# The first loads of an attention kernel issued from two queues, with new issue costs in its planner

## The chip, the cores and the metric

The kernel runs on one core of a Trainium2 chip. The metric is the device time of one execution in microseconds (us). Three runs of the kernel before took 1328.55, 1330.45 and 1333.21 us, so the median is 1330.45 us. All times of single operations below come from one profiled execution, which took 1330.71 us, of which its trace spans 1329.0 us.

The engines are called as the profile calls them: PE is the matrix engine (PEld its weight loads), DVE the vector engine, ACT the scalar engine, POOL the general one, and SP the engine that here does nothing but issue DMAs. A DMA is issued by an engine's instruction stream, in order, and then moves its bytes on the core's 16 DMA engines while the issuing engine goes on.

## The reference

Attention whose heads are mixed before and after the softmax ("talking heads"), then two layers of dense work. The sizes are 4 batches, 12 heads, 448 positions, 64 features a head.

```python
scores = scale * np.matmul(q, k.transpose(0, 1, 3, 2))
scores = np.einsum('bhij,hg->bgij', scores, w_pre)
scores = scores - np.max(scores, axis=-1, keepdims=True)
attn = np.exp(scores)
attn = attn / (np.sum(attn, axis=-1, keepdims=True) + 1e-09)
attn = np.einsum('bhij,hg->bgij', attn, w_post)
attn_out = np.matmul(attn, v)
...
h = x @ w_in                      # x: attn_out as 1792 x 768
x = (h * np.cos(h)) @ w_out
...
h = np.maximum(np.maximum(x @ w1, x @ w2), x @ w3)
return h @ w_out2
```

## The kernel before

Each batch's 448 query rows are cut into four score blocks of 120, 110, 110 and 110 rows (`SBLK`), 16 score blocks in all. For each score block n the work goes in this order.

- `qget` and `kget` load the queries and keys of a head pair (two heads) once per batch: the queries in two DMAs of 64 partitions, the keys in one of 128. Each pair is therefore three DMAs of 112, 112 and 224 KB, and a batch has six pairs.
- `qk` (line 675) multiplies one head pair into two PSUM banks. There are four such banks in rotation ("ps", called `ps` and `mps` in the trace), so two pairs fill them.
- `evac` (lines 677 to 680; the copy itself is line 613) copies one head's scores from PSUM to an SBUF tile `s`, on ACT or DVE. There are six `s` tiles. The tile is free again when its send has landed.
- `send` (line 687) is a DMA from SBUF to SBUF that lays one head's rows out so that ten query rows of all twelve heads stand in the 120 partitions of `t`. A score block needs twelve sends, 210 KB each in the 120-row blocks.
- For each group of ten query rows (a "block", 45 a batch): `thigh` and `tlow` cut `t` into two parts (ACT or DVE, then DVE or POOL), `mix1` multiplies them with the first head mixture (lines 703 to 705), `rowmax` and `soft` do the softmax, `wscale` and `mix2` the second mixture (line 731), `keep` copies it out.
- After two score blocks `av` (line 753) multiplies with the values, which `vget` loads.

The order of all this is not the order of the code. `Plan.run` builds it while the program is being made: every operation has a rank, the engines that may run it with a cost in us, the operations it comes after, and the buffers it takes. The planner keeps a clock for each of T (PE), A (ACT), V (DVE), P (POOL) and D (the DMA queue of SP) and emits operations one by one, each on the engine that would finish it first. `LATENCY` is added to an operation's cost before its users may start: 0.12 for ACT, 2.479 for D. What the planner emits is each engine's fixed instruction order; on the chip only semaphores hold an instruction back.

One kind of semaphore matters here. Eight completion counters (`DMAHW0` to `DMAHW7`) go round over the DMAs in the planner's order, whichever engine issues them. A DMA is not issued before the DMA that used its counter last, the eighth before it, has landed.

In the kernel before, all loads and sends are issued by SP; ACT issues none. The first mixture's weights come from three small loads: `wget` (line 629) fetches `w_pre`, `w_post` and `same_row` (tile `blk`), and `wmix` (lines 635 to 643) makes the weights from them on DVE.

After the attention the two dense layers follow, in an order that is written out by hand; the planner already interleaves the first products of the first layer with the last score blocks.

Of the kernel before, what the change touches and what calls it, by code (L numbers as in the profile page):

```python
# [16 lines left out]
B, H, S, D = 4, 12, 448, 64  # L17
# [513 lines left out]
class Plan:  # L531
# [4 lines left out]
    def __init__(self):  # L536
        self.ops, self.takers, self.frees = {}, {}, {}

    def add(self, key, rank, run, engines, after=(), takes=(), frees=(), behind=()):


        assert key not in self.ops, key
        self.ops[key] = (rank, run, engines, list(after), list(takes), list(behind))
        for x in frees:
            self.frees.setdefault(x, []).append(key)

    def run(self, places):
# [8 lines left out]
        while open_:  # L556
# [21 lines left out]
            t, _, _, eng, key = min(picks)  # L578
# [3 lines left out]
            if eng == "-":  # L582
                done[key] = t
            else:
                d = engines[eng]
                free[eng] = t + d
                done[key] = t + d + self.LATENCY[eng]
            run(eng)
# [8 lines left out]
def attention(ctx, tc, q, k, v, w_pre, w_post, same_row, xT, tp, mlps):  # L597
    nc = tc.nc
# [28 lines left out]

    def wget(x, _):
        nc.sync.dma_start(blk if x == 2 else wraw[:, x, :], (w_pre, w_post, same_row)[x])

# [15 lines left out]

    def kget(b, hp, _):
        live["k", b, hp] = kp.tile([128, S], F32, name="k")
        nc.sync.dma_start(live["k", b, hp], k[b, hp])

# [33 lines left out]

    def send(n, h, _):
        b, _, m, nt = score[n]
        nc.sync.dma_start(live["t", n][h:P:H, :nt, :], live.pop(("s", n, h))[:m])

# [97 lines left out]
    for x in range(3):  # L786
        add(wget, (x,), -50.0, {"D": 0.45})
    add(wmix, (0,), -39.0, {"V": 0.8}, [("wget", 0), ("wget", 2)], takes=["s"], frees=[("s", ("wmix", 0))])
    add(wmix, (1,), -39.0, {"V": 0.2}, [("wget", 1), ("wget", 2)])
    for n in range(NS):  # L790
        b, _, m, nt = score[n]
        for hp in range(HP):
            r = rank_qk[n, hp]
            if n % per == 0:
                early = 8.0 if b else 20.0
                add(qget, (b, hp), r - early, {"D": 0.9}, turn=True, takes=["q"])
                add(kget, (b, hp), r - early, {"D": 0.65}, turn=True, takes=["k"])
            last = [("k", ("kget", b, hp)), ("q", ("qget", b, hp))] if n % per == per - 1 else []
            add(qk, (n, hp), r, {"T": 1.04}, [("qget", b, hp), ("kget", b, hp)], turn=True, takes=["ps", "ps"], frees=last)
            for h in (2 * hp, 2 * hp + 1):  # L800
                add(evac, (n, h), r, {"A": 0.424, "V": 0.535}, [("qk", n, hp)], turn=True, takes=["s"], frees=[("ps", ("qk", n, hp))])
                if h == 0:
                    plan.add(("new_t", n), r, partial(new_t, n), {}, [("evac", n, 0)], takes=["t"])
                add(send, (n, h), r, {"D": 0.65}, [("evac", n, h), ("new_t", n)], turn=True, frees=[("s", ("evac", n, h))])

# [149 lines left out]
```

## Time and profile before

| | |
|---|---|
| median of three runs | 1330.45 us |
| profiled execution | 1330.71 us, its span 1329.0 us |
| PE busy | 1273.8 us, 96% of the span |
| DVE, ACT, POOL busy | 1029.5, 763.5, 289.0 us |
| one head pair's loads | 448 KB in three DMAs |
| one send of the first score block | 210 KB |

In a row of the timeline the first number is the start in us from the span's start, the second the duration, and the bracket at the end is how long the engine stood idle before it and what ended that wait. "SPq" is a DMA issue by SP: its duration is the issue, not the transfer. Equal instructions that follow each other on an engine are merged, with their count after "x", and the duration then runs from the first to the end of the last.

### The profile page before, as it was taken

Reading aid. Unit: us, or ns where it says so; the run is one execution under the profiler, and the core shown is the slowest. Engines: PE = TensorE matmul, PEld = TensorE weight load, DVE = VectorE, ACT = ScalarE, POOL = GpSimd, SP = SyncE. Lnnn points to the kernel's source line nnn. Section 1 sums busy time; section 2 is a strip of 40 time slices with the busy share of each in tenths; the row PEclk is TensorE's granted clock in tenths of the full one; section 3 lists DMA queues with packets and bytes.
Section 4 is the critical chain, followed back from the end, with each engine's and each line's share of the span. In section 5 each row is a group of like instructions: output and inputs, shape, how many; then the busy total and the mean of one; then the engine's idle time right before and its main releaser. Section 6 shows DMA issues by size and latency. Waiting matters only on the chain. (4 is left out here: it accounts for less than half of the span.)

```text
span 1329.0 us, 20579 instructions
## 1 busy us (share of the span) xinstructions
PE 1273.8 (96%) x7002; PEld 1055.8 (79%) x7002; DVE 1029.5 (77%) x2180; ACT 763.5 (57%) x1684; POOL 289.0 (22%) x258
## 2 busy tenths in 40 slices
PE   7999999999999989999999999999989999999998
PEld 2677666776777668888988888889989898989998
DVE  1888797887878797999989998989795645966445
ACT  3877676776777677765545555555553445344430
POOL 0000010000101036121201111111116636256350
PEclk7999999999999999999999999999999999999999
DMA  7652444444343335544343444433102212232112
GB/s 206 195 167 89 125 130 141 124 118 128 110 127 108 123 108 169 141 137 138 101 131 108 119 123 120 131 104 90 54 13 72 72 48 72 79 100 72 48 54 83
DMA packets 84766, 145.44 MB, mean 109 GB/s; under 512 B 9174, under 2 KB 67638, under 8 KB 84662
## 3 DMA queue, kind: packets, MB, share of 16 engines
q1 hardware_dynamic: 84661, 144.14, 36.9%
q8 instruction: 55, 0.90, 0.3%
q14 instruction: 50, 0.40, 0.1%
HBM read 84.95 MB, written 20.45 MB: 79 GB/s over the span
## 5 line engine op out<-in xcount | busy, mean ns | idle before, releaser
L190 PE MATMUL ps<-x,w 128*128 128x448 f32 x708 | 265.3, 375 | 26.0 <-DVE r L229 19.1
L192 PE MATMUL ps<-x,w 128*128 128x448 f32 x708 | 261.6, 370 | 2.4 <-DVE x L358 1.2
L191 PE MATMUL ps<-x,w 128*128 128x448 f32 x708 | 261.7, 370 | 0.0
L731 PEld LDWEIGHTS aps<-w2s,e 120*112 120x112 f32 x1440 | 165.0, 177 | 50.0 <-issue 20.0
L190 PE MATMUL ps<-gh,w 128*128 128x448 f32 x528 | 193.4, 366 | 0.0
L191 PE MATMUL ps<-gh,w 128*128 128x448 f32 x528 | 193.1, 366 | 0.0
L192 PE MATMUL ps<-gl,w 128*128 128x448 f32 x528 | 193.0, 365 | 0.0
L731 PE MATMUL aps<-w2s,e 120*112 120x120 f32 x1440 | 180.2, 271 | 7.8 <-DVE w2s L726 4.9
L337 POOL TENSOR_TENSOR w<-wf,w 128x384 fp32r<-128x384 f32 x126 | 139.8, 1133 | 191.0 <-ACT w L336 131.2
L149 POOL TENSOR_TENSOR w<-wf,w 128x384 fp32r<-128x384 f32 x88 | 99.2, 1138 | 367.5 <-ACT w L146 225.5
L190 PEld LDWEIGHTS ps<-x,w 128*128 128x128 f32 x708 | 134.6, 190 | 48.3 <-DVE r L229 27.0
L192 PEld LDWEIGHTS ps<-x,w 128*128 128x128 f32 x708 | 134.6, 190 | 15.2 <-DVE x L358 1.6
L191 PEld LDWEIGHTS ps<-x,w 128*128 128x128 f32 x708 | 134.7, 190 | 11.1 <-POOL w L149 0.2
L709 DVE TENSOR_REDUCE nm<-mps 120x1 f32<-120x448 f32 x180 | 111.5, 620 | 36.6 <-PE mps L705 33.1
L714 ACT ACTIVATE e<-mps,nm 120x448 f32<-120x448 f32 x180 | 114.8, 638 | 40.0 <-DVE nm L709 31.4
L698 POOL TENSOR_TENSOR tl<-t,th 120x448 fp32r<-120x448 f32 x22 | 26.3, 1196 | 438.2 <-ACT th L613 361.2
L331 DVE TENSOR_TENSOR wf<-wf 128x384 f32<-128x384 f32 x72 | 61.0, 856 | 63.6 <-DMA wf<-w 49.7
L336 ACT CAST w<-wf 128x384 fp32r<-128x384 f32 x126 | 61.2, 515 | 80.7 <-PE ps L192 31.9
L192 PEld LDWEIGHTS ps<-gl,w 128*128 128x128 f32 x528 | 99.1, 188 | 8.6
L190 PEld LDWEIGHTS ps<-gh,w 128*128 128x128 f32 x528 | 99.1, 188 | 8.6 <-issue 0.3
L191 PEld LDWEIGHTS ps<-gh,w 128*128 128x128 f32 x528 | 99.1, 188 | 8.3
L613 ACT CAST th<-t 120x448 fp32r<-120x448 f32 x167 | 94.6, 568 | 19.0 <-DMA t<-s 6.1
(102 smaller groups left out, 2272.3 us busy)
## 6 DMA issues: line engine op xcount, KB each, us to landing
t<-s SPq DMA_DIRECT2D x144, 192.5 KB
wf<-w SPq DMA_DIRECT2D x96, 192.0 KB
wraw<-in_w_out_dram SPq DMA_DIRECT2D x44, 384.0 KB
wraw<-in_w_dram SPq DMA_DIRECT2D x36, 384.0 KB
wraw<-in_w_in_dram SPq DMA_DIRECT2D x32, 384.0 KB
t<-s SPq DMA_DIRECT2D x48, 210.0 KB
w<-wf SPq DMA_DIRECT2D x48, 192.0 KB
q<-in_q_dram SPq DMA_DIRECT2D x48, 112.0 KB
```

Of the source, the lines that this page charges most:

```text
L149: nc.gpsimd.tensor_sub(lo, chunks(o["f"]), f32(hi))
L190: mm(w[0], x[0], start=first, stop=False)
L191: mm(w[1], x[0], start=False, stop=False)
L192: mm(w[0], x[1], start=False, stop=last)
L331: f(raw[x], raw[l], raw[r])
L336: nc.scalar.copy(hi, w)
L337: nc.gpsimd.tensor_sub(lo, w, f32(hi))
L613: copy = lambda eng, *a: nc.scalar.copy(*a) if eng == "A" else any_of[eng].tensor_copy(*a)
L698: any_of[eng].tensor_sub(live["tl", i], live["t", n][:P, t, :], f32(live["th", i]))
L709: nc.vector.tensor_reduce(nm, live["m", i][:P], axis=AX.X, op=ALU.max, negate=True)
L714: nc.scalar.activation(e, live["m", i][:P], AF.Exp, bias=live["nm", i], scale=1.0, accum_out=z)
L731: nc.tensor.matmul(ps[:JC, j], live["e", i][:, j * JC:(j + 1) * JC], live["w2s", i], start=True, stop=True)
```

## The change

The keys of the first batch and the three small weight loads are issued by ACT instead of SP. The sends of the first score block may be issued by either, as the planner finds; all later sends stay on SP. The planner's costs of a load of queries (0.9 to 1.1), of keys (0.65 to 0.62) and of a send (0.65 to 0.85) are changed for every score block, so the whole order of the attention is planned anew. An operation marked `lands` gets the DMA's latency in the plan even where ACT issues it. The small loads' rank goes from -50 to -30.

```diff
@@ Plan
-                done[key] = t + d + self.LATENCY[eng]
+                done[key] = t + d + self.LATENCY["D" if key in self.lands else eng]
@@ attention
-    def wget(x, _):
-        nc.sync.dma_start(blk if x == 2 else wraw[:, x, :], (w_pre, w_post, same_row)[x])
+    def begin(eng):
+        return nc.scalar if eng == "A" else nc.sync
+
+    def wget(x, eng):
+        begin(eng).dma_start(blk if x == 2 else wraw[:, x, :], (w_pre, w_post, same_row)[x])
...
-    def kget(b, hp, _):
+    def kget(b, hp, eng):
         live["k", b, hp] = kp.tile([128, S], F32, name="k")
-        nc.sync.dma_start(live["k", b, hp], k[b, hp])
+        begin(eng).dma_start(live["k", b, hp], k[b, hp])
...
-    def send(n, h, _):
+    def send(n, h, eng):
         b, _, m, nt = score[n]
-        nc.sync.dma_start(live["t", n][h:P:H, :nt, :], live.pop(("s", n, h))[:m])
+        begin(eng).dma_start(live["t", n][h:P:H, :nt, :], live.pop(("s", n, h))[:m])
...
-        add(wget, (x,), -50.0, {"D": 0.45})
+        add(wget, (x,), -30.0, {"A": 0.45}, lands=True)
...
-                add(qget, (b, hp), r - early, {"D": 0.9}, turn=True, takes=["q"])
-                add(kget, (b, hp), r - early, {"D": 0.65}, turn=True, takes=["k"])
+                add(qget, (b, hp), r - early, {"D": 1.1}, turn=True, takes=["q"])
+                add(kget, (b, hp), r - early, {"D": 0.62} if b else {"A": 0.62}, turn=True, takes=["k"], lands=True)
...
-                add(send, (n, h), r, {"D": 0.65}, [("evac", n, h), ("new_t", n)], turn=True, frees=[("s", ("evac", n, h))])
+                add(send, (n, h), r, {"D": 0.85} if n else {"A": 0.85, "D": 0.85}, [("evac", n, h), ("new_t", n)], turn=True, lands=True, frees=[("s", ("evac", n, h))])
```

ACT's first instructions before. A name with a number is one tile; "waits" lists the semaphores that the instruction waits for, `PE_49` and the like being the progress of an engine and `DMAHW4_49` completion counter 4.

```order
L613 ACT_TABLE_LOAD
L613 COPY s_159<-ps_152 120x448 [waits PE_49]
L613 COPY s_173<-mps_165 120x448 [waits PE_49]
L613 COPY s_186<-ps_179 120x448 [waits PE_49]
L613 COPY s_215<-mps_192 120x448 [waits DMAHW5_49,DVE_49,PE_49]
L613 COPY s_219<-mps_193 120x448 [waits DMAHW6_49,PE_49]
```

ACT's first instructions now, with the six loads of keys, the three small loads and the first sends (lines 655, 635 and 693 of the changed file).

```order
L655 DMA k_149<-in_k_dram 128x448
L655 DMA k_154<-in_k_dram 128x448 [waits DMAHW0_49]
L655 DMA k_156<-in_k_dram 128x448 [waits DMAHW2_49]
L635 DMA wraw_132<-in_w_pre_dram 120x12 [waits DMAHW4_49]
L635 DMA wraw_132<-in_w_post_dram 120x12 [waits DMAHW6_49]
L635 DMA blk_133<-in_same_row_dram 120x10 [waits DMAHW0_49]
L616 ACT_TABLE_LOAD
L616 COPY s_177<-ps_162 120x448 [waits PE_49]
L693 DMA t_179<-s_175 10x12x448 [waits DMAHW4_49,DVE_49]
L693 DMA t_179<-s_177 10x12x448 [waits DMAHW7_49,Activation_49]
L693 DMA t_179<-s_191 10x12x448 [waits DMAHW5_49,DVE_49]
L693 DMA t_179<-s_194 10x12x448 [waits DMAHW6_49,DVE_49]
```

Ahead of ACT's table load and of its first copy there now stand nine DMAs, five of which wait for a counter. The last of them, `blk`, waits for counter 0, which then belongs to the fifth load of keys, `k_154`.

The rest of ACT's share of the first score block now (the names ending in 214, 227, 230, 237, 245, 249 are the heads 5, 7, 8, 9, 10 and 11).

```order
L616 COPY s_214<-ps_185 120x448 [waits DVE_49,PE_49]
L693 DMA t_179<-s_214 10x12x448 [waits DMAHW7_49,Activation_49]
L616 COPY s_227<-mps_197 120x448 [waits PE_49]
L616 COPY s_230<-ps_219 120x448 [waits PE_49]
L693 DMA t_179<-s_227 10x12x448 [waits DMAHW1_49,Activation_49]
L693 DMA t_179<-s_237 10x12x448 [waits DMAHW3_49,DVE_49]
L693 DMA t_179<-s_245 10x12x448 [waits DMAHW1_49,DVE_49]
L693 DMA t_179<-s_249 10x12x448 [waits DMAHW2_49,DVE_49]
```

Nine of the twelve sends are ACT's. The one of head 10 (`s_245`) waits for counter 1, which head 7's send (`s_227`) took two sends earlier.

SP's issues before, from the last loads to the first sends.

```order
L649 DMA k_190<-in_k_dram 128x448 [waits DMAHW1_49]
L629 DMA wraw_132<-in_w_pre_dram 120x12 [waits DMAHW2_49]
L629 DMA wraw_132<-in_w_post_dram 120x12 [waits DMAHW3_49]
L629 DMA blk_133<-in_same_row_dram 120x10 [waits DMAHW4_49]
L687 DMA t_169<-s_159 10x12x448 [waits DMAHW5_49,Activation_49]
L687 DMA t_169<-s_161 10x12x448 [waits DMAHW6_49,DVE_49]
L687 DMA t_169<-s_173 10x12x448 [waits DMAHW7_49,Activation_49]
```

SP's issues now, from the seventh DMA on (line 660 is a load of queries, 664 one of values).

```order
L660 DMA q_158<-in_q_dram 64x448 [waits DMAHW7_49]
L660 DMA q_167<-in_q_dram 64x448 [waits DMAHW1_49]
L660 DMA q_167<-in_q_dram 64x448 [waits DMAHW2_49]
L660 DMA q_181<-in_q_dram 64x448 [waits DMAHW3_49]
L660 DMA q_181<-in_q_dram 64x448 [waits DMAHW5_49]
L693 DMA t_179<-s_188 10x12x448 [waits DMAHW6_49,DVE_49]
L664 DMA v_201<-in_v_dram 112x512 [waits DMAHW0_49]
L664 DMA v_209<-in_v_dram 112x512 [waits DMAHW1_49]
```

SP now issues the queries alone, and of the sends only those of heads 2, 6 and 8; five loads of values moved ahead between the first and the second of these. The second half of the fifth pair's queries (`q_167`) waits for counter 2, which is the sixth load of keys on ACT's queue.

## Rows read from the trace of the kernel before

**Rows 1.** Busy time by stretch: stretch, its length, engines' busy us, PEclk, DMA share, GB/s

```profile
0.00:5.00 5.00, 0.00 (x0) 0.00 (x0) 0.00 (x0) 1.28 (x1) 0.20 (x4) 1.00 0.44 123
5.00:10.00 5.00, 4.11 (x10) 1.46 (x12) 1.25 (x2) 1.07 (x2) 0.00 (x0) 1.00 0.86 241
10.00:15.00 5.00, 4.53 (x12) 1.20 (x10) 0.62 (x1) 0.53 (x1) 0.00 (x0) 1.00 0.97 204
15.00:20.00 5.00, 1.98 (x6) 1.28 (x6) 1.16 (x5) 1.60 (x3) 0.00 (x0) 0.70 0.65 208
30.00:38.00 8.00, 7.99 (x19) 3.62 (x19) 3.90 (x13) 5.02 (x12) 1.57 (x1) 0.53 0.74 227
60.00:450.00 390.00, 384.55 (x2670) 272.81 (x2669) 318.50 (x902) 284.60 (x712) 19.90 (x17) 1.00 0.41 123
450.00:500.00 50.00, 42.07 (x288) 32.70 (x288) 44.91 (x106) 38.14 (x91) 15.37 (x13) 0.97 0.41 128
500.00:600.00 100.00, 94.76 (x470) 84.87 (x466) 87.95 (x152) 69.51 (x143) 34.98 (x29) 1.00 0.50 148
600.00:1329.00 729.00, 702.58 (x3389) 638.73 (x3387) 550.00 (x947) 339.29 (x673) 214.44 (x192) 0.99 0.30 88
```

**Rows 2.** Timeline of PE at the start: first products of keys and queries

```profile
5.07 1.85 PE L675 MATMUL ps<-k,q 64*120 64x448 f32 x4 [5.07 <-DMA k<-in_k_dram]
7.45 1.85 PE L675 MATMUL mps<-k,q 64*120 64x448 f32 x4 [0.53 <-DMA k<-in_k_dram]
9.59 1.98 PE L675 MATMUL ps<-k,q 64*120 64x448 f32 x4 [0.30 <-issue]
11.90 1.89 PE L675 MATMUL mps<-k,q 64*120 64x448 f32 x4 [0.33 <-DMA k<-in_k_dram]
13.94 1.11 PE L675 MATMUL ps<-k,q 64*120 64x448 f32 x4
18.06 2.58 PE L675 MATMUL mps<-k,q 64*120 64x448 f32 x4 [3.02 <-ACT s L613]
...
31.86 0.73 PE L703 MATMUL mps<-th,w1h 120*120 120x448 f32 x1
```

**Rows 3.** Timeline of SP's issues at the start

```profile
0.74 1.23 SPq L654 DMA_DIRECT2D q<-in_q_dram  x2
2.01 0.59 SPq L649 DMA_DIRECT2D k<-in_k_dram  x1
2.63 1.10 SPq L654 DMA_DIRECT2D q<-in_q_dram  x2
...
7.33 0.58 SPq L649 DMA_DIRECT2D k<-in_k_dram  x1
...
12.45 0.41 SPq L629 DMA_DIRECT2D blk<-in_same_row_dram  x1
12.98 5.25 SPq L687 DMA_DIRECT2D t<-s  x6
18.28 0.50 SPq L658 DMA_DIRECT2D v<-in_v_dram  x1
18.88 10.20 SPq L687 DMA_DIRECT2D t<-s  x11
```

**Rows 4.** Timeline of ACT at the start

```profile
0.73 1.28 ACT L613 ACT_TABLE_LOAD   x1 [0.73 <-PEq L946]
6.92 0.53 ACT L613 COPY s<-ps 120x448 f32<-120x448 f32 x1 [4.90 <-PE ps L675]
...
18.21 0.53 ACT L613 COPY s<-mps 120x448 f32<-120x448 f32 x1 [0.20 <-DMA t<-s]
...
29.07 0.57 ACT L613 CAST th<-t 120x448 fp32r<-120x448 f32 x1 [0.85 <-DMA t<-s]
```

**Rows 5.** Timeline of DVE at the start

```profile
15.84 0.28 DVE L643 TENSOR_TENSOR w2t<-wraw,blk 120x120 f32<-120x120 f32 x1 [3.61 <-DMA blk<-in_same_row_dram]
...
16.54 0.28 DVE L637 TENSOR_TENSOR s<-wraw,blk 120x120 f32<-120x120 f32 x1 [0.32 <-DMA t<-s]
...
29.13 0.39 DVE L613 CAST th<-t 120x448 fp32r<-120x448 f32 x1 [6.05 <-DMA t<-s]
29.43 0.62 DVE L613 COPY s<-ps 110x448 f32<-110x448 f32 x1
```

**Rows 6.** Busy time by stretch: six us of sends, five of large loads

```profile
23.00:29.00 6.00, 6.00 (x13) 2.65 (x12) 0.07 (x1) 2.67 (x5) 0.00 (x0) 0.50 0.66 234
510.00:515.00 5.00, 5.00 (x26) 4.59 (x25) 2.41 (x4) 4.35 (x9) 2.85 (x3) 1.00 1.05 391
```

**Rows 7.** What PE waited for from 450 to 500 us: total, times, longest

```profile
PE aps L731 <- DVE w2s L726: 2.9, 4, 1.5
PE mps L703 <- ACT e L714: 2.7, 2, 1.8
```

More of the change, by code (lines that the diff above doesn't have):

```diff
@@ L536, in __init__, with add @@
     def __init__(self):
-        self.ops, self.takers, self.frees = {}, {}, {}
-    def add(self, key, rank, run, engines, after=(), takes=(), frees=(), behind=()):
+        self.ops, self.takers, self.frees, self.lands = {}, {}, {}, set()
+    def add(self, key, rank, run, engines, after=(), takes=(), frees=(), behind=(), lands=False):
         assert key not in self.ops, key
         self.ops[key] = (rank, run, engines, list(after), list(takes), list(behind))
+        if lands:
+            self.lands.add(key)
         for x in frees:
```

## The prediction

> **What bounds the kernel now.** I read the busy time by stretch first [rows 1]. From 60 us on PE is what bounds the kernel: busy 384.6 of 390 us until 450, and 702.6 of 729 after 600. Two stretches stand out. From 450 to 600 us, where the attention hands over to the dense layers, PE idles 7.9 and 5.2 us. In the first 38 us little useful work is done: PE stands still for 5 us, then runs products that wait for one another, and from 15 us on its granted clock falls to the lower of its two levels (0.50, 1.2 GHz) and is still there in most of the stretch from 30 to 38 (0.53). The change works on this start. After it PE has no slack, so a microsecond by which the first `mix1` starts earlier or later should show in the end time nearly whole.
>
> The timelines of the start say what that first `mix1` (31.86 us [rows 2]) waits for. SP issues loads without a pause from 0.74 to 12.9 us, then the twelve sends of the first score block with one load of values between them [rows 3]. The cut of the first block starts on ACT when the last of these sends lands, at 29.07 us [rows 4].
>
> Is it SP's issuing or the transfers that limit the loads? The first four head pairs' products start at 5.07, 7.45, 9.59 and 11.90 us, 2.28 us apart [rows 2]. SP issues a pair's three DMAs every 1.77 us (keys at 2.01 and, three pairs later, 7.33 [rows 3]). The distance from a pair's issue of keys to its product grows from 3.06 us (2.01 to 5.07) to 4.57 us (7.33 to 11.90). So the transfers fall behind the issue: a backlog is building in the DMA engines, whose share is 0.86 and 0.97 in these stretches [rows 1]. PE and the copies add little to this, since the waits in front of these products name the keys.
>
> **The change, part by part.** What leaves SP is six loads of keys at 0.59 us, three small loads (1.3 us in all) and nine sends at 0.87 us (5.25 / 6 [rows 3]), 12.7 us of issuing. The same work now stands in ACT's stream, in order with ACT's table load and copies.
>
> *The loads.* At 2.28 us a pair, the transfers and not SP set the time, so I give the second queue no gain there. The Trainium skill, DMA: Bandwidth & Descriptors, section "Issuing engines are not separate DMA queues", says that DMAs of all issuing engines run on the same 16 DMA engines and that a second issuer saves only the time of issuing. The trace agrees as far as it goes (2.28 against 1.77 us); the sum is the same without it.
>
> *ACT's first copy.* A new wait stands here. ACT may issue `blk` only when the fifth load of keys has landed (counter 0), and behind `blk` stand the table load and ACT's first copy. Before, all five first pairs had landed by 13.94 us, when the fifth product starts without a recorded wait [rows 2]. The fifth keys now come with one load of queries less ahead of them, 112 of a pair's 448 KB or 0.57 us: 13.4 us. Then 0.41 for issuing `blk`, 1.28 for the table load and 0.53 for the copy [rows 3, 4] give 15.6 us. Before, ACT's table load was over at 2.0 us and its first copy ran at 6.92 [rows 4]. PE's third pair needs the bank that this copy empties; its second half moves from about 9.6 to 15.6 us, and the pairs behind it in PE's order move too, since nothing passes it.
>
> *The first block's sends.* ACT's first sends can go at 15.6 and 16.5 us; SP's first went at 12.98 before. Now follow the counters. SP's second half of the fifth pair's queries waits for the sixth keys: 13.4 plus 224 KB at the same pace (1.14), so 14.5; three issues of queries at 0.55 and SP sends head 2 at 16.2. A send that goes into nearly empty queues lands after 3.56 us (issued 12.98, its waiter on DVE released at 16.54 [rows 3, 5]), the second after 4.35 (issued about 13.86, its waiter on ACT runs at 18.21 [rows 3, 4]), and the twelfth, in full queues, after 5.6 (issued about 23.5, cut at 29.07). Head 2 therefore lands at 19.8, and ACT's send of head 4, which waits for that counter, is issued from 19.8 to 20.6. Then in ACT's order: copy 5, send 5, copies 7 and 8, send 7 at 23.1 (0.53 a copy, 0.87 a send). Head 10's send waits for the counter of head 7's. With values and the next block's first loads on the way I take 4.35 for that, so 27.5; head 11's goes at 28.3 and lands at 32.7 us. Before it was 29.07, so the first block is complete 3.6 us later.
>
> *From there to the first `mix1`.* DVE casts (0.39) and copies a head that PE still needs (0.62) [rows 5]; PE's half pair takes about 0.9 (half of 1.85 [rows 2]), so `mix1` starts at 34.6 us in place of 31.86: **2.7 us later**. PE's clock was granted in full in the 10 to 15 us stretch and fell in the next, after a gap of 3.02 us in front of the product at 18.06 [rows 1, 2]; the new gap, from about 11.5 to 15.6, is in the same place and I give it no price.
>
> *The rest of the attention.* The new issue costs order everything anew. From 60 to 450 us there is no stall to take away: PE idles 5.4 us in 390, and the DMA engines are at a share of 0.41 [rows 1]. In the handover PE waits 2.9 us for DVE's `w2s` and 2.7 for ACT's `e` [rows 7]; a new order may halve or lengthen this by half, -3 to +3 us. I take 0, because the same operations stand there and nothing in the rows favours a sign. The dense layers after 600 us keep their written order.
>
> *Bounds of the start.* From below: if the loads ran at the 391 GB/s of the stretch at 510 us [rows 6], a pair would take 1.17 us and the fifth keys would land 3.75 x 1.11 = 4.2 us sooner; with 3.56 for every landing (another 1.6) the start is 3.1 us earlier than before. From above: at 5.6 us for the three landings in the chain (heads 2, 7 and 11) it adds 2.0 + 1.25 + 1.25 = 4.5, 7.2 us later than before. I take 2.7, near the middle, because the rates of [rows 2] are of these very loads.
>
> The sum: 1330.71 (profiled execution) + 2.7 + 0 = 1333.4. The median lies 0.26 below that execution, so 1333.2; I say **1333 us**.
>
> **The rivals.** *Slower: the counters with full queues.* Same mechanism, higher price. If the three landings take 5.6 us, as the twelfth send's did, the end is at 1330.45 + 7.2 = 1337.7. It decides from 1.3 us over my sum, some 0.45 us more for each landing. For it: six loads of values now run beside the sends, where one did. Against it: the sends are spread wider, so the queues should be shorter than at 23 us.
>
> *Faster: issuing was the limit.* SP's queue is solid with issues from 0.74 to 18.8 us [rows 3], and two issuers halve that. Then loads come at 1.1 us a pair (SP's two queries [rows 3]), the fifth keys land near 9.2, and ACT's first copy ends at 11.4. If no counter held the sends, ACT's last six copies and sends of the chain would follow without pause: nine sends at 0.87 and three more copies at 0.53 after 11.4, so the last is issued by 20.8 and lands 24.4 us; `mix1` would start at 26.3, 5.5 us sooner, and the end would be 1325. The Trainium skill, Perfetto Trace Analysis, section "DMA Optimizations", says that balancing DMAs over several issuing engines may help where descriptor generation is the bottleneck, that is where the engine is busy with issue slices. Against it: the growing distance in [rows 2, 3], and the stretch of nothing but sends from 23 to 29 us, where the DMA share stays at 0.66 and 234 GB/s [rows 6] while landings take 5.6 us, so transfers queue up there as well. If only the loads are faster and the counters hold, the start is about 3 us earlier, 1327.4, still within what can be told from no change.
>
> *The new order decides.* The handover at 450 to 500 us has 7.9 us of idle PE and a DVE that is busy 44.9 of 50 us [rows 1]. A copy or two more on DVE there goes straight onto the path: with the start's 2.7 and +4 the end is 1337, with -4 it is 1329.
>
> That the change does not do what it says is excluded: the order shows the DMAs on ACT's queue.
>
> **How the numbers follow.** My forecast (a start later by 1 to 4 us, the rest as before) 0.45; slower by full queues 0.25; faster by issue 0.15; the new order decides 0.15, a little more than half of it upwards. About 0.3%, 4.0 us, is what a measurement of this kernel can tell from no change: faster means under 1326.5, slower over 1334.4. Faster: most of the third case, 0.12, and 0.03 from the order. Slower: 0.23 of the second, 0.08 of the order and 0.05 from the forecast's upper end, 0.36. Same: the rest, 0.49. The range for 8 in 10 goes from 1328, which takes in faster loads with held sends nearly whole, to 1338, the full price of the counters. The likeliest case alone is 1331.5 to 1334.5.
>
> **What would show it.** In the profile after, ACT's table load should begin near 13.8 us and its first copy near 15; PE's third pair should be split by a gap of some 4 us; the sends of heads 4 and 10 should be issued just when heads 2 and 7 land; the first cut should run near 32.7 and the first `mix1` near 34.6; from 60 to 450 us PE should idle 4 to 7 us. I am wrong if head pairs' products come much less than 2.2 us apart, if the first cut runs before 29 us, or if the handover's idle time moves by more than 3 us.

## The result, and the profile after

The changed kernel takes 1336.88 us (median of six runs, 1336.41 to 1340.41) against 1330.72 us of the kernel before (six runs): a ratio of 1.0054, 95% interval 1.0041 to 1.0067. It is slower by 6.2 us. The profiled execution took 1336.51 us, its span 1334.7 us. The time lies in the prediction's range of 1328 to 1338, near its upper end. The likeliest case (1331.5 to 1334.5) did not happen; the rival "the counters with full queues" had said slower, at 1337.7.

Busy time by stretch, changed kernel (columns as in [rows 1]):

```profile
0.00:5.00 5.00, 1.10 (x2) 0.47 (x2) 0.00 (x0) 0.00 (x0) 0.20 (x4) 1.00 0.63 175
5.00:10.00 5.00, 4.49 (x7) 1.42 (x6) 1.25 (x2) 0.14 (x1) 0.00 (x0) 1.00 1.06 256
10.00:15.00 5.00, 4.67 (x11) 1.80 (x10) 2.31 (x7) 1.67 (x2) 0.00 (x0) 1.00 0.66 169
12.00:37.00 25.00, 15.63 (x33) 5.59 (x32) 5.27 (x12) 3.10 (x6) 0.00 (x0) 0.61 0.76 213
15.00:20.00 5.00, 0.00 (x0) 0.00 (x0) 0.62 (x1) 0.00 (x0) 0.00 (x0) 0.75 0.98 231
30.00:38.00 8.00, 5.51 (x11) 1.33 (x8) 1.48 (x4) 2.46 (x5) 0.22 (x1) 0.50 0.64 202
60.00:450.00 390.00, 387.57 (x2698) 277.10 (x2698) 321.99 (x917) 286.86 (x715) 24.50 (x20) 1.00 0.42 125
450.00:500.00 50.00, 41.00 (x273) 31.72 (x269) 44.94 (x108) 33.87 (x80) 20.05 (x16) 0.97 0.39 124
500.00:600.00 100.00, 96.18 (x494) 86.53 (x494) 86.88 (x152) 72.02 (x148) 35.54 (x30) 1.00 0.50 149
600.00:1329.00 729.00, 703.06 (x3384) 638.12 (x3383) 553.79 (x950) 339.15 (x675) 214.95 (x192) 0.99 0.30 87
```

Two things stand against [rows 1]. From 15 to 20 us PE does nothing at all (0.00, before 1.98), while the DMA engines are at a share of 0.98. From 60 to 450 us it is the other way round: PE idles 2.4 us of 390, before 5.4.

ACT at the start, from the timeline of the changed kernel (compare [rows 4]; "ACTq" is a DMA issue by ACT):

```profile
0.73 4.02 ACTq L655 DMA_DIRECT2D k<-in_k_dram  x6
...
9.49 0.33 ACTq L635 DMA_DIRECT2D blk<-in_same_row_dram  x1
9.86 1.28 ACT L616 ACT_TABLE_LOAD   x1 [9.86 <-DMA k<-in_k_dram]
11.15 0.53 ACT L616 COPY s<-ps 120x448 f32<-120x448 f32 x1
11.64 9.25 ACTq L693 DMA_DIRECT2D t<-s  x4
20.99 0.53 ACT L616 COPY s<-ps 120x448 f32<-120x448 f32 x1 [9.31 <-DMA v<-in_v_dram]
...
22.94 8.80 ACTq L693 DMA_DIRECT2D t<-s  x4
...
37.14 0.56 ACT L616 CAST th<-t 120x448 fp32r<-120x448 f32 x1 [2.08 <-DMA t<-s]
```

ACT needs 9.25 us for four sends, from 11.64 on, and its second copy waits behind them. The last four sends take 8.80 us. An issue alone is 0.79 to 0.92 us on ACT; the rest is waiting. The cut of the first block comes at 37.14, 8.1 us later than the 29.07 of [rows 4]. In the second profile of the changed kernel it comes at 35.28, where the second profile of before has 28.79:

```profile
35.28 0.56 ACT L616 CAST th<-t 120x448 fp32r<-120x448 f32 x1 [1.43 <-DMA t<-s]
```

SP's issues in the same time (compare [rows 3]):

```profile
0.74 11.99 SPq L660 DMA_DIRECT2D q<-in_q_dram  x12
12.85 0.97 SPq L693 DMA_DIRECT2D t<-s  x1
13.87 3.49 SPq L664 DMA_DIRECT2D v<-in_v_dram  x5
20.66 3.46 SPq L693 DMA_DIRECT2D t<-s  x2
24.81 0.32 SPq L664 DMA_DIRECT2D v<-in_v_dram  x1
25.19 1.18 SPq L660 DMA_DIRECT2D q<-in_q_dram  x2
27.83 0.36 SPq L655 DMA_DIRECT2D k<-in_k_dram  x1
```

Nine loads stand here before the first block's last send: six of values, two of queries and one of keys for the next batch. In the kernel before there is one, of values [rows 3].

PE and DVE in the same timeline (compare [rows 2, 5]):

```profile
3.90 1.82 PE L681 MATMUL ps<-k,q 64*120 64x448 f32 x2 [3.90 <-DMA q<-in_q_dram]
...
21.57 1.10 PE L681 MATMUL ps<-k,q 64*120 64x448 f32 x1 [6.90 <-ACT s L616]
...
39.88 0.73 PE L709 MATMUL mps<-th,w1h 120*120 120x448 f32 x1
...
502.49 3.20 PE L759 MATMUL ps<-a,v 112*64 112x220 f32 x32
```

```profile
25.06 0.62 DVE L616 COPY s<-ps 120x448 f32<-120x448 f32 x1 [8.66 <-DMA t<-s]
```

The first product comes 1.2 us earlier (3.90, before 5.07). Then PE stands for 6.9 us because ACT's second copy is late, and DVE's copy waits 8.66 us for a send to land, since a copy needs one of six `s` tiles and a tile is free again only when its send has landed. The first `mix1` starts at 39.88 in place of 31.86.

Both kernels were profiled a second time. The points of the way to the end, in us; "values done" is the end of the last product with the values (for the changed kernel 502.49 + 3.20):

| | first `mix1` | values done | end of span |
|---|---|---|---|
| before, two profiles | 31.86, 31.09 | 502.7, 501.9 | 1329.0, 1328.2 |
| changed, two profiles | 39.88, 38.03 | 505.7, 504.2 | 1334.7, 1334.2 |
| mean delay | 7.5 | 2.6 | 5.8 |

So the start loses 7.5 us, the rest of the attention gives back 4.9, and the dense layers lose another 3.2. A reading of the start from a single profile is good to 1 to 2 us.

### The profile page after: what moved, and what is told of

It reads as the page before. It is cut to its first block, busy times and chain, and to the rows that moved or that the text cites. A ratio compares the mean times of both kernels' runs of the same rounds, so it can differ in the third digit from the quotient of the medians.

```text
span 1334.7 us, 20586 instructions
## 1 busy us (share of the span) xinstructions
PE 1275.1 (96%) x7002; PEld 1057.5 (79%) x7002; DVE 1034.3 (77%) x2192; ACT 754.6 (57%) x1667; POOL 297.1 (22%) x263
## 5 line engine op out<-in xcount | busy, mean ns | idle before, releaser
L704 POOL TENSOR_TENSOR tl<-t,th 120x448 fp32r<-120x448 f32 x26 | 32.8, 1263 | 436.7 <-ACT th L616 311.4
L616 ACT CAST th<-t 120x448 fp32r<-120x448 f32 x161 | 90.4, 566 | 13.2 <-DMA t<-s 4.2
```

The costliest lines, as they stand in the source:

```text
L616: copy = lambda eng, *a: nc.scalar.copy(*a) if eng == "A" else any_of[eng].tensor_copy(*a)
L704: any_of[eng].tensor_sub(live["tl", i], live["t", n][:P, t, :], f32(live["th", i]))
```

## The experiments

Each kernel was timed against the kernel before on the same chip, but for two that were only profiled. All profiles are single executions. Where an expectation gives a first `mix1` of a kernel on SP alone (30.3, or 32 to 33 as before), that is the third of its three products; the 40 us of the changed kernel and the times given below are of the first one, 0.5 to 0.9 us earlier.

**Only the new costs.** The kernel before with the three new issue costs; SP issues everything.

```diff
-    add(qget, (b, hp), r - early, {"D": 0.9}, ...)
-    add(kget, (b, hp), r - early, {"D": 0.65}, ...)
+    add(qget, (b, hp), r - early, {"D": 1.1}, ...)
+    add(kget, (b, hp), r - early, {"D": 0.62}, ...)
...
-    add(send, (n, h), r, {"D": 0.65}, ...)
+    add(send, (n, h), r, {"D": 0.85}, ...)
```

> The kernel before with nothing but the new planner costs (queries 1.1, keys 0.62, sends 0.85); every DMA stays on SP. Theory (the loss is the start, where sends on two queues share the DMA engines with five loads of values and hold each other by the completion counters): the start is that of before, first mix1 at 31 to 33 us, and since PE idled 2.4 us in the changed kernel from 60 to 450 us against 5.5 before, the time is 1327 to 1331. Rival (the newly planned order of the whole attention costs the time): first mix1 as before and yet 1335 or more.

Measured: 1327.89 us, ratio 0.9981 (0.997 to 0.9993). The planner now puts no load between the sends. SP and ACT in its timeline:

```profile
12.98 19.19 SPq L687 DMA_DIRECT2D t<-s  x21
```

```profile
27.91 0.56 ACT L613 CAST th<-t 120x448 fp32r<-120x448 f32 x1 [0.84 <-DMA t<-s]
```

The first cut comes 1.2 us earlier than before (27.91 against 29.07), the first `mix1` at 29.82 (its third product at 30.32, a little before the 31 to 33 of the theory). The costs alone are no loss.

**All sends on SP.** The changed kernel, with keys and small loads on ACT as changed, but no send there.

```diff
-    add(send, (n, h), r, {"D": 0.85} if n else {"A": 0.85, "D": 0.85}, ...)
+    add(send, (n, h), r, {"D": 0.85}, ...)
```

> The changed kernel with all sends on SP again; the keys and the three small loads stay on ACT. The planner then puts the values behind the sends by itself. Theory: sends land 3.5 to 5.6 us after their issue as before, first mix1 at 30 to 33 us, time 1326 to 1331. Rival (the nine DMAs ahead of ACT's table load and first copy are what costs): first mix1 stays above 36 and the time above 1334.

Measured: 1325.12 us, ratio 0.9954 (0.9937 to 0.9971), first cut at 27.61, first `mix1` at 29.52. SP and ACT in its timeline:

```profile
12.69 22.10 SPq L693 DMA_DIRECT2D t<-s  x24
```

```profile
27.61 0.56 ACT L616 CAST th<-t 120x448 fp32r<-120x448 f32 x1 [0.58 <-DMA t<-s]
```

This edit alone turns the loss into a gain: it has the lowest median of this study, a little under the theory's range, 5.9 us under the kernel before on the same chip (1330.99) and 11.8 under the changed one's median. With all sends on SP the planner puts the values behind them, so two things went at once, the second queue and the loads among the sends.

**Sends on both queues, nothing beside them.** The changed kernel, in which the values of the first batch and the queries and keys of the second may only go after the first block's last send.

```diff
-    add(qget, (b, hp), r - early, {"D": 1.1}, turn=True, takes=["q"])
+    add(qget, (b, hp), r - early, {"D": 1.1}, [("send", 0, H - 1)] if b == 1 else [], turn=True, takes=["q"])
...
-    add(vget, (b, hp), r - 10.0, {"D": 0.65}, turn=True, takes=["v"])
+    add(vget, (b, hp), r - 10.0, {"D": 0.65}, [] if b else [("send", 0, H - 1)], turn=True, takes=["v"])
```

(The keys get the same condition as the queries.)

> The changed kernel, sends on both queues, but the values of the first batch and the queries and keys of the second may be issued only after the last send of the first score block. Theory: without loads beside them the sends land in 3.5 to 4.5 us instead of 7 and first mix1 starts at 29 to 33 us, time 1327 to 1331. Rival (the order of ACT's stream and the counters alone cost the time, whatever runs beside the sends): sends still go out in bursts with gaps of several us on ACT, first mix1 at 36 or later, time 1334 or more.

Measured: 1327.34 us, ratio 0.9967 (0.9951 to 0.9983), first `mix1` at 31.27. ACT in its timeline:

```profile
11.98 2.67 ACTq L693 DMA_DIRECT2D t<-s  x3
15.31 0.80 ACTq L693 DMA_DIRECT2D t<-s  x1
19.43 0.53 ACT L616 COPY s<-mps 120x448 f32<-120x448 f32 x1 [4.14 <-DMA t<-s]
...
29.32 0.57 ACT L616 CAST th<-t 120x448 fp32r<-120x448 f32 x1 [1.43 <-DMA t<-s]
```

Two issuers push out the first sends faster, but ACT's next copy waits 4.14 us for one to land and free its tile. One part of the theory failed: by the semaphore records of the trace (from a send's issue to its last update) the six sends issued from 12.9 to 16.6 us landed after 6.1 to 7.3 us and not after 3.5 to 4.5, with no load beside them. The first cut comes at 29.32, 1.7 us later than with all sends on SP (27.61), no more than the start varies by from profile to profile. So the second queue brings the sends nothing that can be told; most of the changed kernel's loss is the loads beside them.

**Small loads and sends on SP, keys on ACT.**

```diff
-    add(wget, (x,), -30.0, {"A": 0.45}, lands=True)
+    add(wget, (x,), -50.0, {"D": 0.45})
...
-    add(send, (n, h), r, {"D": 0.85} if n else {"A": 0.85, "D": 0.85}, ...)
+    add(send, (n, h), r, {"D": 0.85}, ...)
```

(The values are held behind the last send, as above.)

> Only the six loads of keys on ACT: the small loads and all sends on SP, values behind the sends, new costs. Theory: two queues bring the first product to 3.9 us as in the changed kernel, ACT's table load is free at some 5 us, SP's first send goes at 9 to 11 us instead of 13, first mix1 at 28 to 31 us, time 1325 to 1329, the fastest of these four. Rival (the loads are bound by transfers and the second queue gives nothing): first mix1 at 31 to 33, time as that of the costs alone.

Measured: 1327.36 us, ratio 0.9977 (0.9963 to 0.9991), first cut at 27.11, first `mix1` at 29.30. The stretch in which the loads run, and SP's first send:

```profile
5.00:10.00 5.00, 5.00 (x8) 1.89 (x8) 0.69 (x2) 2.30 (x3) 0.00 (x0) 1.00 1.08 256
```

```profile
11.81 20.92 SPq L693 DMA_DIRECT2D t<-s  x22
```

The DMA share is 1.08, before 0.86 [rows 1], and the sends begin at 11.81 in place of 12.98. For the loads, the second queue works. Yet of 1.2 us at the first send only 0.8 is left at the first cut (27.11 against the 27.91 of the costs alone) and 0.5 at the first `mix1`, all within what the start varies by. The first send came later than the 9 to 11 us of the theory, and the kernel is not the fastest of the four: in time it cannot be told from the costs alone (1327.89).

**Values among the sends, one queue only.** The kernel with only the new costs, in which the six loads of values go as soon as the first send has been planned. They come to stand behind the fourth.

```diff
-    add(vget, (b, hp), r - 10.0, {"D": 0.65}, turn=True, takes=["v"])
+    add(vget, (b, hp), r - 10.0 if b else -60.0, {"D": 0.65}, [] if b else [("send", 0, 0)], turn=True, takes=["v"])
```

> The kernel costs_only (all on SP, new issue costs; first mix1 at 30.3 us in its own profile, 1327.9 us), with one edit: the six loads of values of the first batch are issued straight behind the fourth send of the first score block. No second queue, no send on ACT. It asks what of the late start of the changed kernel is due to values that stand among the sends, and what to the second queue. Theory (bytes among the sends: a load of values is 229 KB, a send 210 KB, and both share the DMA engines, at the 234 GB/s of the stretch of sends alone in [rows 6]): six loads cost 6 x 229 / 234 = 5.9 us of transfer, landings of the sends issued next to them rise to 7 us or more, the first mix1 comes at 35 to 37 us, the time is about 1333 to 1334. Rival 1 (only SP's time of issuing counts): 6 x 0.58 = 3.5 us, first mix1 near 33.8, 1331. Rival 2 (values do no harm as long as all sends stand on one queue, and the loss of the changed kernel needs the second queue): first mix1 before 31.5, under 1329.

Measured: 1334.03 us, ratio 1.0029 (1.0011 to 1.0046), first `mix1` at 36.03. SP, then ACT and DVE in its timeline, then the stretch up to the first cut:

```profile
12.98 3.55 SPq L687 DMA_DIRECT2D t<-s  x4
16.58 2.99 SPq L658 DMA_DIRECT2D v<-in_v_dram  x6
19.68 21.59 SPq L687 DMA_DIRECT2D t<-s  x20
```

```profile
26.71 0.53 ACT L613 COPY s<-mps 120x448 f32<-120x448 f32 x1 [4.72 <-DMA t<-s]
...
33.97 0.56 ACT L613 CAST th<-t 120x448 fp32r<-120x448 f32 x1 [1.02 <-DMA t<-s]
```

```profile
27.59 0.62 DVE L613 COPY s<-mps 120x448 f32<-120x448 f32 x1 [10.23 <-DMA t<-s]
```

```profile
12.00:34.00 22.00, 14.07 (x30) 5.33 (x26) 1.78 (x6) 5.35 (x11) 0.00 (x0) 0.63 0.73 212
```

This is the decisive run. With everything on SP, six loads put the first cut 6.1 us later (33.97 against 27.91), though SP spends only 2.99 us on issuing them. Their bytes explain it: 6 x 112 x 512 x 4 is 1.38 MB, and at the 212 GB/s of this stretch that is 6.5 us. The rival by issue time (33.8) and the one by which values do no harm without a second queue both fall.

**Loads on SP, sends on both queues.**

```diff
-    add(wget, (x,), -30.0, {"A": 0.45}, lands=True)
+    add(wget, (x,), -50.0, {"D": 0.45})
...
-    add(kget, (b, hp), r - early, {"D": 0.62} if b else {"A": 0.62}, ...)
+    add(kget, (b, hp), r - early, {"D": 0.62}, ...)
```

> The changed kernel with keys and small loads back on SP, while the sends of the first block may still go on both queues (eight of twelve on ACT; the planner leaves four loads of values among them). ACT's first copy no longer stands behind nine DMAs. Theory (the loss is made by values among sends, plus some 2 us for sends on two queues, and not by the loads of keys on ACT): four values cost 4 x 229 KB / 234 GB/s = 3.9 us over the 30.3 of costs_only, and 2 for the two queues, so the first mix1 starts at about 36 us and the time is 1332 to 1335. Rival (the loads of keys and small loads in front of ACT's copies are part of the loss): first mix1 under 33.5, 1329 to 1330.

Measured: 1330.29 us, ratio 1.0 (0.9986 to 1.0013), first cut at 33.59, first `mix1` at 36.52 (third product 37.42). The start is late, as the theory said, and somewhat more. In the trace nine of the twelve sends are ACT's, and three loads of values (0.69 MB, 3.2 us at 212 GB/s) stand ahead of the last of them; the fourth is issued behind it. So the bytes give only part of the delay. Another wait is in ACT's stream: its first two sends take 8.59 us, since the second waits for the counter of the fifth keys, which land at 15.29, and ACT's next copies stand behind it.

```profile
7.58 8.59 ACTq L693 DMA_DIRECT2D t<-s  x2
```

So a late start does not need the keys on ACT's queue. The time is another matter: it is 1.7 us under the theory's range and next to the rival's 1329 to 1330. The start is 4.7 to 5.4 us late, and the end not at all. It comes back in the attention: from the first `mix1` to the end of the values this kernel takes 464.8 us, the kernel before 470.9. Why is what the next runs ask.

**The costs in two halves.** The kernel before with the new costs for the first batch's loads and the first block's sends alone:

```diff
+    add(qget, (b, hp), r - early, {"D": 0.9 if b else 1.1}, ...)
+    add(kget, (b, hp), r - early, {"D": 0.65 if b else 0.62}, ...)
+    add(send, (n, h), r, {"D": 0.65 if n else 0.85}, ...)
```

> The kernel before with the new issue costs for the first batch's keys and queries and the first block's sends only; all later loads and sends keep the old costs; everything on SP. It asks where the gain of costs_only (1327.9 against 1331.0) is made: at the start, or in the order of the later blocks, where PE idled 2.2 us of 390 between 60 and 450 us instead of 5.4. Theory (the start, since values move behind the sends; the later idle time follows from being planned on a later clock of the DMA queue): first mix1 near 30.3, and if the later order is that of before, PE idles about 5 us from 60 to 450 us and the time is 1328 to 1329.5. Rival (the later order makes it): first mix1 near 30.3 but the gain of the median under 1.5 us, because 3 us come back in the later blocks: 1330 to 1331.

and with the new ones for everything later alone:

```diff
+    add(qget, (b, hp), r - early, {"D": 1.1 if b else 0.9}, ...)
+    add(kget, (b, hp), r - early, {"D": 0.62 if b else 0.65}, ...)
+    add(send, (n, h), r, {"D": 0.85 if n else 0.65}, ...)
```

> The other half: the old costs for the first batch's loads and the first block's sends, the new ones for all later loads and sends, everything on SP. One load of values stands among the sends, as before. Theory of the start: first mix1 at 32 to 33 as before, and what the new costs of later blocks give is PE's idle time from 60 to 450 us, 2 to 3 us instead of 5.4, so 1328 to 1330. Rival (the order of the later blocks gives nothing by itself): idle time as before, 1330 to 1331.5.

Measured: the start's costs 1330.1 us, ratio 0.9999 (0.9986 to 1.0011), first cut at 28.21, first `mix1` at 30.96; the later costs 1328.88 us, ratio 0.9987 (0.9972 to 1.0001), first `mix1` at 31.94. The stretch from 60 to 450 us of the first and of the second:

```profile
60.00:450.00 390.00, 383.53 (x2663) 271.75 (x2664) 318.20 (x898) 283.22 (x708) 19.94 (x17) 1.00 0.41 123
```

```profile
60.00:450.00 390.00, 388.11 (x2705) 276.67 (x2704) 320.65 (x917) 285.36 (x715) 20.87 (x17) 1.00 0.42 126
```

The later costs take PE's idle time from 5.4 to 1.9 us; the start's costs leave it at 6.5. What the costs give in the blocks comes from the order of the later blocks, as the second theory said; at the end the interval just reaches 1.0, so a gain there is not shown. For the start's costs the times fit neither case cleanly: the rival had the median right, but not the later blocks, and a start 0.1 to 0.9 us earlier (30.96 against 31.86 and 31.09) is too little to be seen at the end.

**The changed start with the old later costs.** The changed kernel with 0.9, 0.65 and 0.65 for all later batches and blocks.

```diff
-    add(qget, (b, hp), r - early, {"D": 1.1}, ...)
-    add(kget, (b, hp), r - early, {"D": 0.62} if b else {"A": 0.62}, ...)
+    add(qget, (b, hp), r - early, {"D": 0.9 if b else 1.1}, ...)
+    add(kget, (b, hp), r - early, {"D": 0.65} if b else {"A": 0.62}, ...)
...
-    add(send, (n, h), r, {"D": 0.85} if n else {"A": 0.85, "D": 0.85}, ...)
+    add(send, (n, h), r, {"D": 0.65} if n else {"A": 0.85, "D": 0.85}, ...)
```

> The changed kernel with the old issue costs (0.9, 0.65, 0.65) for all batches but the first and all score blocks but the first; the start as changed (keys and small loads on ACT, sends on both queues, five loads of values behind SP's first send). The two halves of the change are thus parted: costs_rest showed the new later costs alone (PE idle 1.9 us of 390 between 60 and 450 us, 0.9987), costs_start the new start costs alone (idle 6.5 us, 0.9999). Theory (the changed kernel loses 8 us at the start and wins back about 3 to 4 in the later blocks through the new costs): first mix1 at 40 us as in the changed kernel, PE idle 5 to 6.5 us from 60 to 450 us, and a time of 1338.5 to 1341. Rival (the gain of the later blocks comes from the late start itself, since work that waited is done with no more gaps, whatever the costs): PE idle 2 to 3 us, and 1335.5 to 1337.5.

Measured: 1337.76 us, ratio 1.0049 (1.003 to 1.0067), first `mix1` at 41.67. The same stretch:

```profile
60.00:450.00 390.00, 382.79 (x2658) 272.96 (x2657) 321.47 (x904) 284.74 (x711) 25.40 (x21) 1.00 0.41 123
```

PE idles 7.2 us here, so the 2.4 of the changed kernel are the later costs' doing and not the late start's. The time lies just above the rival's range and under the theory's. With the later costs (1.0054, 1.0041 to 1.0067) or without them (1.0049, 1.003 to 1.0067), the changed start gives the same time within the intervals: of what they win in the attention nothing can be told at the end, where the intervals leave room for some 2 us.

**Both kernels a second time.**

> The kernel before, word for word, profiled a second time: 1329 to 1333. From the first products of the dense part that all runs share (the 200th of the first layer) to the end it took 704.3 us in its first profile, and 705.3 to 709.4 in the nine others, with stretches at the lower clock of 5 to 10 us of PE time between 600 and 1329. Theory (these dips of the granted clock fall differently in each execution): the dense part takes 706 to 709 us this time. Rival (they belong to the kernel): 704 to 705 again, with dips at the same places (706, 867, 990, 1167 us).

> The changed kernel, word for word, profiled a second time: 1335 to 1339, first mix1 within 0.5 us of 39.88. Dense part 709.0 us in its first profile. Theory (dips differ by execution): anywhere from 704 to 709. Rival (they belong to the kernel): 708.5 to 709.5, with double-length dips at 990 and 1171 us again.

Measured: 1329.99 and 1335.97 us, in one run each. From the end of the values to the end of the span the kernel before takes 826.3 us in both profiles; the changed kernel takes 829.0 and 830.0. In the expectations' measure it is 704.1 after 704.3 us for the kernel before, and 710.2 after 709.0 for the changed one. The theory of varying dips falls for the kernel before; for the changed kernel 710.2 lies just above both ranges. Its first `mix1` came at 38.03, 1.85 us from 39.88, where at most 0.5 was expected. The stretches at the lower clock come at 706 and 1167 us again in the kernel before, but one moved from 867 to 833, and the one at 990 came at 986 and twice as long; in the changed kernel those at 990 and 1171 are of double length both times. They do not make the difference: from 600 to 1320 us they add up to 17 us in both profiles of the changed kernel and in the second of before, and to 14 in the first, and before took 826.3 us both times. So the 3.2 us that the dense layers lose look like a property of the kernel and not of an execution, as far as two profiles each can say. They are not a property of the second queue: in the other kernels the same stretch takes 827.0 to 831.1 us, and the longest is that of the new costs alone. Why they are lost was not tried. The waits of PE from 626 to 700 us, kernel before, then the changed kernel's first and second profile, say where the larger part of it is:

```profile
PE ps L190 <- DVE r L229: 2.5, 3, 1.6
```

```profile
PE ps L190 <- DVE r L229: 5.1, 4, 2.7
```

```profile
PE ps L190 <- DVE r L229: 4.6, 3, 3.5
```

The first dense products wait twice as long for DVE (2.5 us in the second profile of before, too). At 990 us a single wait for DVE's `acc` is 4.9 and 5.2 us long, before 3.7 and 3.4. DVE is behind, but which operation of the new order put it there stays open.

## Why the prediction was right, and where it was wrong

**The mechanism of the start held.** The new wait on ACT, the sends held up in order at their counters, and the mixture that starts when the last send lands: each is in the timelines. The loss is at the start, and the sign of the forecast's sum was right. That a microsecond of the start shows in the end "nearly whole" was not borne out: 7.5 us became 5.8 here, and with the loads on SP 4.7 to 5.4 us became nothing.

**The step that failed is the landing time of the sends: a term of the sum that was mis-sized.** The chain of counters is in the trace. ACT issues head 4's send at 20.11 us, just after head 2's has landed (20.03 by the semaphore records), and head 10's at 29.56, just after head 7's (29.49):

```profile
20.11 0.79 ACTq L693 DMA_DIRECT2D t<-s  x1
...
29.56 2.17 ACTq L693 DMA_DIRECT2D t<-s  x2
```

The landings are what it had wrong. It gave 3.56 us to head 2 and 4.35 to heads 7 and 11; they took 7.2, 6.5 and 6.1 us (in the second profile 7.0, 6.7 and 5.2). It named the loads of values beside them as a reason for the rival only, and even there priced a landing at no more than 5.6 us. That head 2 landed when forecast (20.03, forecast 19.8) is luck: its send was issued 3.3 us earlier and took 3.6 us longer. The start came out at +7.5 us (two profiles) and not +2.7. The loads are shown as the reason by the run with the values on one queue: the send right behind the six loads landed after 6.9 us, and with the same costs and no load among the sends those issued from 17 to 20 us landed after 4.1 to 4.4.

What should have been summed is bytes. Between the first send and the first cut the DMA engines move 211 to 213 GB/s in the three kernels compared, with one load, six or nine among the sends: before 211 from 12 to 29 us, with the values on one queue 212, changed 213 (222 in its second profile; 188 to 211 in the other kernels). At one rate, every load ahead of the last send delays it by its bytes:

| kernel | sends issued by | loads ahead of the last send, MB | first cut, us | later than the first row | MB / 0.212 |
|---|---|---|---|---|---|
| new costs | SP | 0 | 27.91 | | 0 |
| all sends on SP | SP | 0 | 27.61 | -0.3 | 0 |
| start's costs | SP | 0 | 28.21 | 0.3 | 0 |
| small loads and sends on SP | SP | 0 | 27.11 | -0.8 | 0 |
| before | SP | 0.23 | 29.07 | 1.2 | 1.1 |
| before, second profile | SP | 0.23 | 28.79 | 0.9 | 1.1 |
| later costs | SP | 0.23 | 29.14 | 1.2 | 1.1 |
| values among the sends | SP | 1.38 | 33.97 | 6.1 | 6.5 |
| sends alone | both | 0 | 29.32 | 1.4 | 0 |
| loads on SP | both | 0.69 | 33.59 | 5.7 | 3.2 |
| changed | both | 1.84 | 37.14 | 9.2 | 8.7 |
| changed, second profile | both | 1.84 | 35.28 | 7.4 | 8.7 |
| changed, old later costs | both | 2.06 | 38.88 | 11.0 | 9.7 |

(A load of values or of keys is 0.229 MB, one of queries 0.115; the changed kernel has six of values, two of queries and one of keys. Not counted is one send of the next score block, 0.2 MB, that also goes ahead in the changed rows.) On one queue the bytes carry the result within 0.4 us, but for the row whose sends start 1.2 us sooner. With two queues the result is off by -1.3 to +2.5, most where ACT stood at a counter among the loads (loads on SP); what the second queue itself adds cannot be told from this. From the rows on record the sum was to be had: 1.84 less 0.23 MB at the 208 to 234 GB/s of [rows 1, 6] is 6.9 to 7.7 us, where the chain of counters gave 3.6 at the first cut; the two profiles measured 8.1 and 6.5. The table is a fit to single profiles, but the run with the values on one queue is a test of it: no second queue, and no ACT that issues anything.

**The loads.** The prediction gave the second queue no gain, since products came 2.28 us apart and SP issued in 1.77. That was wrong in size: the share rises from 0.86 to 1.06, the fifth keys, for which `blk` waits, land by 9.49 and not at 13.4, and ACT's first copy starts at 11.15, not near 15. The gain did not get past the sends: the first of them moved from 12.98 to 11.64, and the first cut from 29.07 to 37.14. The sentence of the Trainium skill that the prediction cited here (DMA: Bandwidth & Descriptors, section "Issuing engines are not separate DMA queues"), that a second issuer saves only time of issuing, usually little beside the transfer, holds for the sends; for these loads the saving was not little (with keys alone on ACT the sends begin 1.2 us sooner), since the DMA engines had room at 0.86, and the measurement decides.

**The rest of the attention, "0 (-3 to +3)".** It gave back 4.9 us, outside these bounds. The prediction looked for the movement in the handover, where PE's wait for `w2s` grew and the one for `e` shrank (compare [rows 7]):

```profile
PE aps L737 <- DVE w2s L732: 4.7, 5, 1.9
...
PE mps L709 <- ACT e L720: 0.4, 1, 0.4
```

That part was right: 5.1 us for both, before 5.6. But from 60 to 450 us "there is no stall to take away" was wrong. The 5.4 us of idle PE shrank to between 1.9 and 3.8 in every kernel with the new later costs. In the changed kernel that is 3.0 of the 4.9 us (3.9 in the second profile). The traces of the other runs say where the 4.9 come from. From the first `mix1` to the end of the values all eight kernels with the new later costs take 464.8 to 466.9 us, the one with the start of before too (later costs, 466.9). With the old later costs it is 470.9 (before, both profiles), 471.4 (start's costs) and 469.6 (the changed start). So 3.6 to 4.0 of the 4.9 us come with the new later costs, whatever the start; the rest, about 1, comes with the changed start (470.9 to 469.6).

**The dense layers, "keep their written order".** They lost 3.2 us. An unchanged order of code does not mean that the engines arrive at it in the same state; every newly planned order lost here, 0.7 to 4.8 us.

**The rivals.** "The counters with full queues" had the sign and nearly the time (1337.7), but its price, 7.2 us from three landings of 5.6, was right only in sum: sends that share the engines with values landed later than that (up to 8.8 us, head 3's, which DVE's copy waits for), and ACT's first copy came 4 us earlier than that price assumed. Its argument against itself, that sends spread wider would find shorter queues, did not hold. "Issuing was the limit" came near for the loads (fifth keys at 9.2, ACT's first copy over at 11.4; measured 11.68) and was false of the sends, as the sends on both queues show. The end at +5.8 us (of the two profiles) is 7.5 - 4.9 + 3.2: the last two terms, at which the prediction put nothing, cancel in part, and that the time came out in the range and near the rival's is in part luck.

## What to carry to other kernels

Before a DMA is moved or a planner's cost is changed, sum the bytes that the new order puts ahead of the transfer the path waits for, and divide by the rate that this stretch of the trace shows: here each load of values (0.229 MB) ahead of the last send cost about 1 us with everything on one queue. A second queue speeds up transfers where the share shows room and one issuer is the limit (the loads), though that was worth little at the end here, and not where short transfers already wait for one another (the sends); put loads that nobody needs yet behind the transfers that somebody does. When a change to costs replans a whole kernel, measure the costs and the new queue apart: here a gain (all sends on SP, 0.9954) was hidden under a loss.

## What the runs showed of the hardware

The sends leave a third of the DMA engines' time unused. In the stretch of sends alone the share is 0.66 [rows 6]. The Trainium skill, DMA: Bandwidth & Descriptors, section "Why a DMA increments its semaphore by 16 and not by 1", says that a DMA uses the largest number of engines up to 16 that divides the slowest dimension on both sides. For a send (10 partitions of `t`, 120 of `s`) that is 10 of 16, an estimate of 0.63 for the share, and the trace agrees with 0.66. It would explain why a stretch with sends stays near 212 GB/s while large loads reach 391 [rows 6]; no run here changed the shape of a send to show it.

A second surprise is how little an earlier first product is worth: with small loads and sends on SP and the keys on ACT, a first product at 3.88 us in place of 5.07 and sends that start 1.2 us earlier left at most 0.5 us at the first `mix1` and nothing in the time that could be told (1327.36 with the keys on ACT, 1327.89 without).
